# Halved first-layer weights, earlier key additions, and gate work moved across a phase border, in attention followed by a gated mixture of experts

## The chip, the cores and the metric

The kernel runs on one core of one Trainium2 chip. The metric is the device time of one execution in microseconds, given as the median of several runs. The core has five engines that run their own instruction streams: TensorE (PE, matmuls; PEld are its weight loads), VectorE (DVE), ScalarE (ACT), GpSimd (POOL) and SyncE (SP). In this kernel SyncE issues the plain transfers, and GpSimd issues those that change the type (the expert weights).

## The reference

Multi-query attention is computed first: 8 batches, 16 query heads over one key and value head, 384 tokens, head size 64. Its output is 3072 tokens of 1024 features. Each token then picks the best of 4 groups and the best of 4 experts in it, and passes one expert of two layers (1024 to 1024 to 1024); the result is scaled by the product of two softmax weights.

```python
scores = scale * np.matmul(q, k.transpose(0, 1, 3, 2))
scores = scores - np.max(scores, axis=-1, keepdims=True)
attn = np.exp(scores)
attn = attn / (np.sum(attn, axis=-1, keepdims=True) + 1e-09)
out = np.matmul(attn, v)
...
g_logits = x @ w_group                      # 4 groups
g_idx = np.argmax(g_logits, axis=1)
...
e_logits = xg @ w_expert[g]                 # 4 experts in the group
...
h = np.maximum(xg[mask_e] @ w1[g, e], 0.0)
ye = h @ w2[g, e]
out[tok_idx] = combined[:, None] * ye       # combined = g_w * e_w
```

## The kernel before

The kernel goes through 24 **phases**, `p = 3*b + st`: batch `b` (8 of them), tile `st` of 128 tokens (3 per batch). One phase computes the scores and exponentials of its own tile (six key blocks `j`), and the products with the values of the phase before, in turn. In the data most tokens of a batch go to one expert. So the kernel picks one expert per batch by the counts of the batch's first tile, loads its weights, and runs the whole batch through it, in 14 **units** per batch: 8 of the first layer (`h_unit`, 8 matmuls each) and 6 of the second (`y_unit`, 8 matmuls each). From phase 3 on, 4 or 5 such units follow the attention part of each phase (`fill`), as filling work for TensorE. What the chosen experts leave over is put right at the end with the "extra" pair of batch and expert.

Nearly all matmul results stand in one pool of three PSUM buffers, taken by `side`. A matmul that wants a buffer waits until its former content has been read. The instructions of each engine stand in the order in which the code emits them.

```python
ps_s = fast.enter_context(tc.psum_pool(name="ps_s", bufs=3))
ps_m = fast.enter_context(tc.psum_pool(name="ps_m", bufs=1))
...
def side(shape, dtype, name):
    return ps_s.tile(shape, dtype, tag="s", name=name)

def load_w1(w1, e):                       # 4 MB in DRAM, turned to bf16 on the way
    for a in range(2):
        nc.gpsimd.dma_start(out=w1[a * D:(a + 1) * D], in_=w1f[bass.ds(e, 1), a].rearrange("e p k f -> (e p) k f"))

def scores(p, j):
    ps = side([P, 2, CW], FP32, "s")
    ...                                   # 4 matmuls: s <- qT, kT
    nc.scalar.activation(out=t[:], in_=ps[:], func=ACTF.Exp, scale=scale)   # pt

def pre_add(p, j):                        # sum over the key blocks
    if j == 1:
        nc.vector.tensor_add(out=presum[p][:], in0=pt[p, 0][:], in1=pt[p, 1][:])
    else:
        nc.vector.tensor_add(out=presum[p][:], in0=presum[p][:], in1=pt[p, j][:])

# fold_keys(p): VectorE sums presum to 128 x 32 (fold)
# join(p):      4 small matmuls, sm <- fold
# invert(p):    VectorE reciprocal of sm, then spread over the tile by a transpose (rinv)
# values(p, j): 4 matmuls into o
# prep_q(p), prep_k(b): turn queries and keys by a VectorE transpose; turn_q does it on TensorE

def weigh(p):
    nc.vector.tensor_mul(out=xT[b][:, :, ts], in0=o_ps[p]..., in1=rinv[p]...)
    nc.gpsimd.tensor_copy(out=xbf[b][:, :, ts], in_=xT[b][:, :, ts])   # bf16 for the experts
    ...

def gate_a(b, lo, hi):                    # gate products: gps, copied by ScalarE to part
def gate_b(b, lo=0, hi=ST):               # lps <- part, sel
def choose_a(b, ps):                      # VectorE: best group and expert of the first tile
def choose_b(b):
    ps = side([P, GE], FP32, "c1ps")      # expert counts
    nc.tensor.matmul(out=ps[:], lhsT=ones_bf[:], rhs=first[b]..., start=True, stop=True)
    nc.vector.tensor_copy(out=cnt[:], in_=ps[:])
    nc.vector.max_with_indices(out_max=top[:], out_indices=idx[:], in_=cnt[:])
    reg = nc.values_load(idx[0:1, 0:1], engines=(ET.Pool,), ...)
    load_w1(w1, reg)
    nc.gpsimd.dma_start(out=w2[:], in_=w2f[bass.ds(reg, 1)]...)
    ...
def gate_c(b):                            # counts of all three tiles (cps), then gsel

def h_unit(fc):
    ps = side([P, CW], FP32, "hps")
    ...                                   # 8 matmuls: hps <- xbf, w1
    nc.scalar.activation(out=state["h"][:, fc, :], in_=ps[:, 0:S], func=ACTF.Relu)   # hT
def y_unit(st, nh):
    ps = side([P, CW], FP32, "yps")
    ...                                   # 8 matmuls: yps <- w2, hT
    nc.scalar.activation(out=y, in_=ps[:], func=ACTF.Copy, scale=gs_of()[:, st:st + 1])

# ---- the loop ----
for p in range(NP):
    b, st = divmod(p, ST)
    jobs = jobs_gates(0) if p == 2 else []
    ...
    for j in range(3):
        scores(p, j)
    ...                                   # prep_k, turn_q or prep_q
    for j in range(KB):
        if jobs: jobs.pop(0)()
        if p > 0: values(p - 1, j)
        if j == 2 and p > 0: join(p - 1)
        if j + 3 < KB: scores(p, j + 3)
        if j > 0: pre_add(p, j)
        if j == 2 and p > 0: invert(p - 1)
        if j == 3: stats_q(p)
        ...
    if p > 0: weigh(p - 1)
    fold_keys(p)
    ...                                   # st == 2: prep_k(b + 1), stats_k(b + 1)
    if p >= ST:
        jobs = []
        if st == 1: jobs = jobs_gates(b)  # gate_a; gate_b and the choice; the counts
        if p == NP - 1: jobs = [bound_a, bound_b]
        phase(5 if p in FIVES else 4, jobs)   # a unit, then from the second on also a job

join(NP - 1); ...                         # the tail: last values, last gates, 24 units left,
                                          # the extra pair: load_pair, ph <- w1c, py <- w2c
```

Of the kernel before, what the change touches and what calls it, by code (L numbers as in the profile page):

```python
# [21 lines left out]
def kernel(  # L22
# [11 lines left out]
    nc = tc.nc  # L34
    B, H, S, D = q.shape
# [3 lines left out]
    F = moe_w1.shape[3]  # L39
    assert S == 384 and D == 64 and Dm == 1024 and F == 1024 and N == B * S  # L40
    assert H == 16 and G == 4 and Eg == 4
    ST = S // P
# [10 lines left out]
    w1f = moe_w1.rearrange("g e (a ko d) f -> (g e) a d ko f", a=2, d=D)  # L53
# [3 lines left out]
    HC = CW // P  # L57
# [15 lines left out]
    def side(shape, dtype, name):  # L73
        return ps_s.tile(shape, dtype, tag="s", name=name)

    q_raw, k_raw, v_sb, kT, qT, pt, xT, xbf, gsel, wts = {}, {}, {}, {}, {}, {}, {}, {}, {}, {}

    q_todo = []
    q_nat = []
# [15 lines left out]
    def some_q(n=1):  # L95
        for _ in range(n):
            if q_todo:
                q_todo.pop(0)()
# [38 lines left out]
            q_nat.append(qe)  # L137

    def load_w1(w1, e):
        for a in range(2):  # L140
            nc.gpsimd.dma_start(out=w1[a * D:(a + 1) * D], in_=w1f[bass.ds(e, 1), a].rearrange("e p k f -> (e p) k f"))  # L141

    ones_bf = singles.tile([P, P], BF16, name="ones_bf")
    nc.vector.memset(ones_bf[:], 1.0)
# [45 lines left out]
    def load_gw():  # L190
        for a in range(2):
            rows = slice(a * D, (a + 1) * D)
            nc.sync.dma_start(out=gw[rows, :, 0:G], in_=moe_w_group.rearrange("(a ko d) g -> a d ko g", a=2, d=D)[a])
            for g in range(G):
                nc.sync.dma_start(out=gw[rows, :, G + g * Eg:G + (g + 1) * Eg], in_=moe_w_expert[g].rearrange("(a ko d) e -> a d ko e", a=2, d=D)[a])
# [6 lines left out]
    def stats_q(p):  # L202
        junk = pool.tile([P, 2 * CW], BF16, tag="junk", bufs=1, name="junk")
        nc.scalar.activation(out=junk[:].rearrange("p (h n) -> p h n", h=HP), in_=q_of(p), func=ACTF.Square, accum_out=stat_q[:, p:p + 1])  # L204
# [12 lines left out]
    def turn_q(p, nat, copies):  # L217
        qT[p] = pool.tile([P, 2 * CW], FP32, tag="qT", bufs=2, name="qT")
        n = HP // len(copies)
        for i, copy in enumerate(copies):  # L220
            ps = side([P, 2 * CW], FP32, "qps")
            for h in range(n):
                nc.tensor.transpose(out=ps[:, h * P:(h + 1) * P], in_=nat(i * n + h).rearrange("p a d -> p (a d)"), identity=ident[:])
            copy(out=qT[p][:, i * n * P:(i + 1) * n * P], in_=ps[:, 0:n * P])

    def prep_k(b):
        kT[b] = pool.tile([P, S], FP32, tag="kT", name="kT")
        nc.vector.transpose(out=kT[b][:], in_=k_raw[b][:].rearrange("p k d -> p (k d)"))

    def q_of(p):  # L230
        b, st = divmod(p, ST)
        if b == 0:
            return q_raw[0][:, st].rearrange("p h a d -> p h (a d)")
        return q_raw[b][:, :, st * (P // 32):(st + 1) * (P // 32)].rearrange("p h k d -> p h (k d)")

    def prep_q(p):
        qT[p] = pool.tile([P, 2 * CW], FP32, tag="qT", bufs=2, name="qT")
        nc.vector.transpose(out=qT[p][:].rearrange("p (h n) -> p h n", h=HP), in_=q_of(p))  # L238

    def scores(p, j):  # L240
        b = p // ST
        ps = side([P, 2, CW], FP32, "s")
        for c in range(2):
            for a in range(2):
                r = slice(64 * a, 64 * a + 64)
                nc.tensor.matmul(out=ps[64 * c:64 * c + 64, a, :], lhsT=kT[b][r, j * D:(j + 1) * D], rhs=qT[p][r, c * CW:(c + 1) * CW], start=True, stop=True)  # L246
        t = pool.tile([P, 2, CW], FP32, tag="pt", bufs=9, name="pt")
        nc.scalar.activation(out=t[:], in_=ps[:], func=ACTF.Exp, scale=scale)  # L248
        pt[p, j] = t

    def pre_add(p, j):
        if j == 1:
            presum[p] = pool.tile([P, 2, CW], FP32, tag="presum", bufs=1, name="presum")
# [3 lines that stand above are left out]
# [46 lines left out]
    def gate_a(b, lo, hi):  # L303
        n = (hi - lo) * P
        ps = side([P, CW], FP32, "gps")
        for r in range(2):
            for j in range(4):
                ko = 4 * r + j
                nc.tensor.matmul(out=ps[32 * j:32 * j + 32, 0:n], lhsT=gw[:, ko, :], rhs=xT[b][:, ko, lo * P:hi * P], start=(r == 0), stop=(r == 1), tile_position=(0, 32 * j))
        part[b] = part_all  # L310
        nc.scalar.copy(out=part[b][:, lo * P:hi * P], in_=ps[:, 0:n])

    def gate_b(b, lo=0, hi=ST):
        ps = side([P, ST, 32], FP32, "lps")
        for st in range(lo, hi):
            nc.tensor.matmul(out=ps[:, st, :], lhsT=part[b][:, st * P:(st + 1) * P], rhs=sel[:], start=True, stop=True)  # L316
        return ps
# [104 lines left out]
    def first_units(b):  # L422
        def place(st, cs):
            if done[0]:
                y = pool.tile([P, 2 * CW], FP32, tag="pt", bufs=9, name="yt")
            else:
                y = pool.tile([P, CW], FP32, tag="y", bufs=4, name="y")
            return y[:, 0:CW]

        def store(st, cs, y):  # L430
            nc.sync.dma_start(out=outv[b, :, st, cs], in_=y)
        return moe_units(wts[b][0], wts[b][1], xbf[b], lambda: gsel[b], place, store)

    NP = B * ST
# [3 lines left out]
    stats_k(0)  # L438
    turn_k_first()
    turn_q(0, lambda h: q_raw[0][:, 0, h], [nc.scalar.copy, nc.vector.tensor_copy])  # L440
    turn_q(1, lambda h: q_raw[0][:, 1, h], [nc.vector.tensor_copy])
    load_gw()

    units = []
# [2 lines left out]
    def fill(n):  # L447
        while n > 0:
            if not units:
                if begun[0] >= B or begun[0] not in wts:  # L450
                    return
                units.extend(first_units(begun[0]))
                begun[0] += 1
            units.pop(0)()
            n -= 1

    def phase(n, jobs):
        for i in range(n):
            fill(1)
            some_q()  # L460
            if i > 0 and jobs:
                jobs.pop(0)()
        while jobs:
            jobs.pop(0)()

    def gate_both(b):
        ps = gate_b(b)
        choose_a(b, ps)
        gate_logits(b - 1, ps, 1, ST)
        gate_math(b - 1)  # L470

    def count_both(b):
        choose_b(b)
        gate_c(b - 1)

    def jobs_gates(b):
        if b == 0:
            return [lambda: gate_a(0, 0, 1), lambda: choose_a(0, gate_b(0, 0, 1)), lambda: choose_b(0)]
        return [lambda: gate_a(b, 0, ST), lambda: gate_both(b), lambda: count_both(b)]

    bound = {}
    oki = singles.tile([1, 1], I32, name="oki")
# [20 lines left out]
    FIVES = (9, 13, 17, 20)  # L503
# [3 lines that stand above are left out]
        if st == 0 and b + 1 < B:  # L507
            load_q(b + 1)
        for j in range(3):
            scores(p, j)  # L510
        if p == 0:
            prep_k(1)
        elif p == 1:
            turn_q(2, lambda h: q_raw[0][:, 2, h], [nc.scalar.copy])
        elif p == 2:
            turn_q(3, lambda h: q_nat[h // HC][:, h % HC], [nc.scalar.copy])
        elif p < NP - 1:
            prep_q(p + 1)
        for j in range(KB):
            if jobs:  # L520
                jobs.pop(0)()
            if p > 0:
                values(p - 1, j)
            if j == 2 and p > 0:
                join(p - 1)
            if j + 3 < KB:
                scores(p, j + 3)
            if j > 0:
                pre_add(p, j)
            if j == 2 and p > 0:  # L530
                invert(p - 1)
            if j == 3:
                stats_q(p)
            if p < 4 and 0 < j < 5:
                some_q()
        assert not jobs
        if p > 0:
            weigh(p - 1)
        fold_keys(p)
        if st == 1 and b + 1 < B:  # L540
            if b > 0:
                load_k(b + 1)
            load_v(b + 1)
        if st == 2 and b + 1 < B:
            if b > 0:
                prep_k(b + 1)
            stats_k(b + 1)
        if p >= ST:
            jobs = []
            if st == 1:  # L550
                jobs = jobs_gates(b)
            if p == NP - 1:
                jobs = [bound_a, bound_b]
            phase(5 if p in FIVES else 4, jobs)

    done[0] = True
    join(NP - 1)
# [253 lines left out]
```

## Time and profile before

The median of 3 runs is 494.3 us (493.04 to 494.57). One profiled execution spans 491.4 us.

| part of the profile | before |
|---|---|
| TensorE clock granted, mean | 0.993 |
| scores, TensorE (L246), 1152 matmuls | 141.9 us busy |
| values, TensorE (L285), 1152 matmuls | 140.6 us busy |
| first expert layer (L401), 512 matmuls | 90.9 us busy |
| second expert layer (L409), 384 matmuls | 86.7 us busy |
| exponentials, ScalarE (L248), 144 | 142.1 us busy, 1026 ns each |
| key additions, VectorE (L254, L256), 120 | 145.7 us busy, 1215 ns each |
| weight transfers by GpSimd | 27, 37.84 MB written |

A line of the profile's time order reads: start in us, duration in us, engine, line of the kernel, operation, output and inputs by the names in the code, shapes, and the number of instructions merged; in square brackets stands the idle time of the engine before it and what ended it. A line of waits reads: engine, what waited, for whom, then the total in us, how often, and the longest. TensorE instructions are pipelined, so a merged group can seem longer than the distance to the next one; distances between starts are safer.

### The profile page before, as it was taken

The numbers are of one execution on the slowest core, as the hardware profiler recorded it, in microseconds if no ns is written. First come the engines' busy times: TensorE is split into PE (matmuls) and PEld (weight loads), VectorE is DVE, ScalarE is ACT, GpSimd is POOL, SyncE is SP. The second block draws the span as 40 slices with busy tenths as digits, with TensorE's granted clock in tenths as the row PEclk, the third lists the DMA queues.
The fourth block names the chain that finished last, engine by engine and source line by source line (L and its number), as shares of the span: only waits on it lengthen the run. The fifth ranks groups of instructions, "written<-read, shape, count | busy, mean of one in ns | idle before, by whom it ended". The sixth has DMA issues, their size and how long they took to land. (4 is left out here: it accounts for less than half of the span.)

```text
span 491.4 us, 9357 instructions
## 1 busy us (share of the span) xinstructions
PE 466.2 (95%) x3828; PEld 202.7 (41%) x3828; DVE 307.9 (63%) x487; ACT 247.8 (50%) x346; POOL 48.0 (10%) x64
## 2 busy tenths in 40 slices
PE   7999698999999998999999999999999999999993
PEld 6333244333344334434434334433434434445651
DVE  4779737856777847866677756855686675734200
ACT  2966263664456463565456464565465455423231
POOL 1002000200010000200010002000010002001000
PEclk9999899999999999999999999999999999999998
DMA  8797992996949595996789386977599303985990
GB/s 161 93 118 130 218 187 36 158 245 169 126 66 213 135 222 65 154 211 175 129 119 208 106 187 114 192 146 187 120 155 209 119 21 102 200 190 150 238 261 29
DMA packets 146242, 74.52 MB, mean 152 GB/s; under 512 B 120443, under 2 KB 120443, under 8 KB 146192
## 3 DMA queue, kind: packets, MB, share of 16 engines
q0 software_dynamic: 19008, 37.84, 42.6%
q1 hardware_dynamic: 126384, 35.81, 36.0%
q8 instruction: 32, 0.52, 0.4%
q10 hardware_dynamic: 800, 0.20, 0.2%
q14 instruction: 18, 0.15, 0.1%
HBM read 92.62 MB, written 19.40 MB: 228 GB/s over the span
## 5 line engine op out<-in xcount | busy, mean ns | idle before, releaser
L248 ACT ACTIVATE pt<-s 128x1024 f32<-128x1024 f32 x144 | 142.1, 1026 | 69.7 <-PE s L246 68.5
L246 PE MATMUL s<-qT,kT 64*64 64x512 f32 x1152 | 141.9, 595 | 2.3 <-ACT hT L402 1.7
L285 PE MATMUL o<-pt,v 64*64 64x512 f32 x1152 | 140.6, 590 | 1.2 <-DVE xT L296 1.2
L256 DVE TENSOR_TENSOR presum<-presum,pt 128x1024 f32<-128x1024 f32 x96 | 116.6, 1215 | 7.9 <-DVE presum L254 0.5
L401 PE MATMUL hps<-xbf,w 128*128 128x384 bf16 x512 | 90.9, 330 | 5.4 <-POOL xbf L297 5.0
L409 PE MATMUL yps<-w,hT 128*128 128x512 bf16 x384 | 86.7, 379 | 0.0
L285 PEld LDWEIGHTS o<-pt,v 64*64 64x64 f32 x1152 | 43.4, 133 | 78.7 <-issue 74.9
L401 PEld LDWEIGHTS <-w 128*128 128x128 bf16 x512 | 49.1, 100 | 50.3 <-issue 21.5
L254 DVE TENSOR_TENSOR presum<-pt 128x1024 f32<-128x1024 f32 x24 | 29.1, 1214 | 61.2 <-ACT pt L248 61.1
L402 ACT ACTIVATE hT<-hps 128x384 bf16<-128x384 f32 x64 | 31.3, 489 | 71.2 <-PE hps L401 71.1
L246 PEld LDWEIGHTS s<-qT,kT 64*64 64x64 f32 x1152 | 39.8, 133 | 63.6 <-issue 51.4
L297 POOL CAST xbf<-xT 128x1024 bf16<-128x1024 f32 x24 | 25.0, 1042 | 332.9 <-DVE xT L296 332.9
L409 PEld LDWEIGHTS <-hT 128*128 128x128 bf16 x384 | 36.3, 98 | 49.3 <-issue 8.9
L410 ACT ACTIVATE y<-yps,gsel 128x512 f32<-128x512 f32 x36 | 24.8, 688 | 48.9 <-PE yps L409 41.8
L296 DVE TENSOR_TENSOR xT<-o,rinv 128x1024 f32<-128x1024 f32 x24 | 29.2, 1218 | 3.6 <-PE o L285 3.6
L275 DVE STREAM_TRANSPOSE rinv<-rc 128x1024 f32<-128x1024 f32 x24 | 29.9, 1246 | 0.8
L260 DVE TRANSPOSE_TENSOR_REDUCE fold<-presum 128x32 f32<-128x1024 f32 x24 | 29.6, 1235 | 0.0
L273 DVE RECIPROCAL rc<-sm 128x32 f32<-128x32 f32 x24 | 8.6, 358 | 29.6 <-PE sm L268 29.5
L238 DVE STREAM_TRANSPOSE qT<-qraw 128x1024 f32<-128x1024 f32 x20 | 24.3, 1215 | 2.0 <-DMA qraw<-in_q_dram 1.7
L204 ACT ACTIVATE junk<-qraw 128x1024 bf16<-128x1024 f32 x21 | 22.0, 1049 | 0.0
L141 POOL DMA_DIRECT2D w<-in_moe_w_dram x18 | 12.6, 706 | 69.8 <-DVE gsel L389 43.5
L351 DVE COPY L<-lps 128x20 f32<-128x20 f32 (+1 forms) x16 | 3.0, 186 | 25.5 <-PE lps L316 25.5
(147 smaller groups left out, 187.9 us busy)
## 6 DMA issues: line engine op xcount, KB each, us to landing
w<-in_moe_w_dram POOLq DMA_DIRECT2D x18, 1024.0 KB, 12.9
w<-in_moe_w_dram POOLq DMA_DIRECT2D x9, 2048.0 KB, 23.9
qraw<-in_q_dram SPq DMA_DIRECT2D x56, 192.0 KB, 5.0
out_dram<-y SPq DMA_DIRECT2D x36, 256.0 KB, 4.4
x_bf<-xbf SPq DMA_DIRECT2D x8, 768.0 KB, 3.7
out_dram<-yt SPq DMA_DIRECT2D x12, 256.0 KB, 6.1
v<-in_v_dram SPq DMA_DIRECT2D x16, 96.0 KB, 2.6
k<-in_k_dram SPq DMA_DIRECT2D x28, 48.0 KB, 3.3
```

The source lines that it names most:

```text
L246: nc.tensor.matmul(out=ps[64 * c:64 * c + 64, a, :], lhsT=kT[b][r, j * D:(j + 1) * D], rhs=qT[p][r, c * CW:(c + 1) * CW], start=True, stop ...
L248: nc.scalar.activation(out=t[:], in_=ps[:], func=ACTF.Exp, scale=scale)
L254: nc.vector.tensor_add(out=presum[p][:], in0=pt[p, 0][:], in1=pt[p, 1][:])
L256: nc.vector.tensor_add(out=presum[p][:], in0=presum[p][:], in1=pt[p, j][:])
L260: nc.vector.tensor_reduce(out=fold[p][:], in_=presum[p][:].rearrange("p a (n i) -> p (a n) i", i=32), axis=AX, op=OP.add, apply_transpose= ...
L275: nc.vector.transpose(out=t[:].rearrange("p (b i) -> p b i", i=32), in_=rc[:].rearrange("p c b -> p (c b)").unsqueeze(2).to_broadcast([P, ...
L285: nc.tensor.matmul(out=o_ps[p][64 * a:64 * a + 64, c, :], lhsT=v_sb[b][r, j, :], rhs=pt[p, j][r, a, :], start=(j == 0), stop=(j == KB - 1))
L296: nc.vector.tensor_mul(out=xT[b][:, :, ts], in0=o_ps[p][:].rearrange("p c (h n) -> p (c h) n", n=P), in1=rinv[p][:].rearrange("p (h n) -> ...
L297: nc.gpsimd.tensor_copy(out=xbf[b][:, :, ts], in_=xT[b][:, :, ts])
L401: nc.tensor.matmul(out=ps[:, 0:S], lhsT=w1[:, ko, fc * P:(fc + 1) * P], rhs=xb[:, ko, :], start=(ko == 0), stop=(ko == KO - 1))
L402: nc.scalar.activation(out=state["h"][:, fc, :], in_=ps[:, 0:S], func=ACTF.Relu)
L409: nc.tensor.matmul(out=ps[:], lhsT=state["h"][:, fo, st * P:(st + 1) * P], rhs=w2[:, fo, nh * CW:(nh + 1) * CW], start=(fo == 0), stop=(fo ...
```

## The change

Four things are moved. Nothing is added or taken away in what is computed.

1. The first-layer weights `w1` are loaded in four transfers (two halves of F, each in two partition halves) in place of two, so that the first four units of a batch need the first half alone.
2. The key additions are emitted as their tiles appear: two ahead of the loop over `j`, three in it, two steps earlier than before. VectorE can then add while it would have waited for the join. At the start, the TensorE turns of the first queries are moved too: the second behind the first scores, the third and fourth from the head of their phases to the fourth step of the loop.
3. The gate products and the choice (`gate_a`, then `gate_b` with `choose_a`) come after the last two units of the phase with `st == 1`, in place of after the second and third.
4. The expert counts (`count_both`: `c1ps`, the index, the load of the weights, `cps`, `gsel`) leave that phase, and come first in the filling part of the next one (`st == 2`), ahead of its units.

```diff
     def load_w1(w1, e):
-        for a in range(2):
-            nc.gpsimd.dma_start(out=w1[a * D:(a + 1) * D], in_=w1f[bass.ds(e, 1), a].rearrange("e p k f -> (e p) k f"))
+        for c in range(2):
+            fs = slice(c * F // 2, (c + 1) * F // 2)
+            for a in range(2):
+                nc.gpsimd.dma_start(out=w1[a * D:(a + 1) * D, :, fs], in_=w1f[bass.ds(e, 1), a, :, :, fs].rearrange("e p k f -> (e p) k f"))
...
     turn_q(0, lambda h: q_raw[0][:, 0, h], [nc.scalar.copy, nc.vector.tensor_copy])
-    turn_q(1, lambda h: q_raw[0][:, 1, h], [nc.vector.tensor_copy])
...                        # phase() is taken out; its loop stands below
-        return [lambda: gate_a(b, 0, ST), lambda: gate_both(b), lambda: count_both(b)]
+        return [lambda: gate_a(b, 0, ST), lambda: gate_both(b)]
...
         for j in range(3):
             scores(p, j)
+            if p == 0 and j == 0:
+                turn_q(1, lambda h: q_raw[0][:, 1, h], [nc.vector.tensor_copy])
         if p == 0:
             prep_k(1)
-        elif p == 1:
-            turn_q(2, lambda h: q_raw[0][:, 2, h], [nc.scalar.copy])
-        elif p == 2:
-            turn_q(3, lambda h: q_nat[h // HC][:, h % HC], [nc.scalar.copy])
-        elif p < NP - 1:
+        elif 2 < p < NP - 1:
             prep_q(p + 1)
+        if jobs:
+            jobs.pop(0)()
+        for j in (1, 2):
+            pre_add(p, j)
         for j in range(KB):
-            if jobs:
-                jobs.pop(0)()
             if p > 0:
                 values(p - 1, j)
             if j == 2 and p > 0:
                 join(p - 1)
             if j + 3 < KB:
                 scores(p, j + 3)
-            if j > 0:
-                pre_add(p, j)
+            if 0 < j < 4:
+                pre_add(p, j + 2)
             if j == 2 and p > 0:
                 invert(p - 1)
             if j == 3:
                 stats_q(p)
+                if p == 1:
+                    turn_q(2, lambda h: q_raw[0][:, 2, h], [nc.scalar.copy])
+                elif p == 2:
+                    turn_q(3, lambda h: q_nat[h // HC][:, h % HC], [nc.scalar.copy])
+            if jobs:
+                jobs.pop(0)()
...
         if p >= ST:
-            jobs = []
+            n = 5 if p in FIVES else 4
+            if st == 2 and b > 0:
+                count_both(b)
+            steps = {}
             if st == 1:
-                jobs = jobs_gates(b)
+                gate_a_, gate_b_ = jobs_gates(b)
+                steps = {n - 2: gate_a_, n - 1: gate_b_}
             if p == NP - 1:
-                jobs = [bound_a, bound_b]
-            phase(5 if p in FIVES else 4, jobs)
+                steps = {1: bound_a, 2: bound_b}
+            for i in range(n):
+                fill(1)
+                some_q()
+                if i in steps:
+                    steps[i]()
```

More of the change, by code (lines that the diff above doesn't have):

```diff
@@ L455, in fill @@
             n -= 1
[L457 to L461, printed above, removed]
-                jobs.pop(0)()
-        while jobs:
-            jobs.pop(0)()
     def gate_both(b):
@@ L510 @@
             scores(p, j)
+            if p == 0 and j == 0:
+                turn_q(1, lambda h: q_raw[0][:, 1, h], [nc.vector.tensor_copy])
         if p == 0:
             prep_k(1)
-        elif p == 1:
-            turn_q(2, lambda h: q_raw[0][:, 2, h], [nc.scalar.copy])
-        elif p == 2:
-            turn_q(3, lambda h: q_nat[h // HC][:, h % HC], [nc.scalar.copy])
-        elif p < NP - 1:
+        elif 2 < p < NP - 1:
             prep_q(p + 1)
+        if jobs:
+            jobs.pop(0)()
+        for j in (1, 2):
+            pre_add(p, j)
         for j in range(KB):
-            if jobs:
-                jobs.pop(0)()
             if p > 0:
```

## The prediction

> **What bounds the kernel now.** I read the busy shares first, then TensorE's own waits, then TensorE in order of time, then VectorE in two stretches, and last the DMA in windows of 3 us near the end.
>
> ```profile
> PE 466.2 (95%) x3828; PEld 202.7 (41%) x3828; DVE 307.9 (63%) x487; ACT 247.8 (50%) x346; POOL 48.0 (10%) x64
> ```
>
> TensorE works 466.2 of 491.4 us, so a change that adds no matmuls can win or lose only in TensorE's gaps, 25 us, and in cold clock. Some 7.8 us of them lie behind the last matmul (483.6). The waits (total, times, longest) name most of the others:
>
> ```profile
> PE hps L401 <- POOL xbf L297: 5.0, 2, 4.3
> PE cps L378 <- DVE ohe L365: 2.8, 6, 0.5
> PE s L246 <- ACT hT L402: 1.7, 5, 0.3
> PE gps L309 <- ACT hT L402: 1.7, 3, 0.6
> PE o L285 <- DVE xT L296: 1.2, 1, 1.2
> ```
>
> The 4.3 us is the first expert matmul, at 57.12. Its weights are not late: the weight load in front of it ran at 53.25. It waits for GpSimd's cast (56.02, 1.04 us), and that for VectorE, which from 37 us on has no gap:
>
> ```profile
> 49.81 1.25 DVE L275 STREAM_TRANSPOSE rinv<-rc 128x1024 f32<-128x1024 f32 x1
> 50.98 3.84 DVE L256 TENSOR_TENSOR presum<-presum,pt 128x1024 f32<-128x1024 f32 x3
> 54.74 1.22 DVE L296 TENSOR_TENSOR xT<-o,rinv 128x1024 f32<-128x1024 f32 x1
> 55.88 1.24 DVE L260 TRANSPOSE_TENSOR_REDUCE fold<-presum 128x32 f32<-128x1024 f32 x1
> ```
>
> So phases 1 to 3, which have no expert units, are bound by VectorE. From phase 4 on TensorE is the bound, and VectorE finishes some 2 us behind it in each phase. The phase with st = 2 of batch 1, whose values end on TensorE at 94.40, shows that:
>
> ```profile
> 86.06 1.25 DVE L238 STREAM_TRANSPOSE qT<-qraw 128x1024 f32<-128x1024 f32 x1
> 91.06 0.36 DVE L273 RECIPROCAL rc<-sm 128x32 f32<-128x32 f32 x1 [1.31 <-PE sm L268]
> 92.62 3.84 DVE L256 TENSOR_TENSOR presum<-presum,pt 128x1024 f32<-128x1024 f32 x3
> 96.39 1.22 DVE L296 TENSOR_TENSOR xT<-o,rinv 128x1024 f32<-128x1024 f32 x1
> 98.68 0.53 DVE L228 STREAM_TRANSPOSE kT<-k 128x384 f32<-128x384 f32 x1
> ```
>
> At the end the DMA matters (window: us, busy of each engine, clock, DMA share, GB/s):
>
> ```profile
> 432.00:435.00 3.00, 3.00 (x27) 1.08 (x20) 0.81 (x1) 0.00 (x0) 0.00 (x0) 1.00 1.13 214
> 441.00:444.00 3.00, 3.00 (x16) 1.38 (x15) 1.78 (x12) 1.05 (x2) 0.00 (x0) 1.00 0.00 0
> 477.00:480.00 3.00, 3.00 (x58) 3.00 (x56) 0.00 (x0) 0.94 (x2) 0.00 (x0) 1.00 0.89 313
> 480.00:483.00 3.00, 3.00 (x17) 1.27 (x15) 0.00 (x0) 1.29 (x2) 0.00 (x0) 1.00 0.04 16
> ```
>
> The last batch's weights (issued at 414.05) keep the queues full till about 439; then comes a lull; then the extra pair's weights, issued from 448.61 and 452.7 and landing up to 26.6 us later (tile view), so at about 479.3. The last matmuls `py`, which need them, begin at 479.98: 0.7 us to spare.
>
> [...]after the gap of 4.3 us the windows 58 to 62 show clock 0.52 and 0.63, and the first 32 expert matmuls took 6.97 us (57.12 to 64.09), where 40 later ones take 6.61 (at 313), so 32 take 5.3; after the gap of 1.2 us at 43.6 nothing of the kind. [...]weights alone fill the share to 1.1 at 200 to 214 GB/s. So splitting by F gives order, not speed.
>
> **The change part by part.**
> *Halves of F.* 36 issues of 0.7 us on GpSimd for 18; GpSimd is 10% busy. No expert matmul of before waited for weights: 0.
>
> *Start.* The second query turn moves behind the first scores, so TensorE no longer stands 1.2 us for that query (9.20), but ScalarE's exponentials follow at 0.92 us each, and I get only about 0.8 us on VectorE's first sum.
>
> *Key additions.* In phase 1 VectorE stood 0.83 us for `sm`, in phase 2 2.14 us for `lps`, with additions it could have done. From the first sum of phase 1 (21.25 before, 20.2 now) I walk the new order with the trace's pitches: addition 1.25, reciprocal 0.39, spread 1.17, weighing 1.14, fold 1.16, first choice 1.3, turn 1.15. A phase is 10.15. Phase 2 starts at 30.3 and ends at 41.8 (before 45.78); phase 3 needs 1.15 + 4x1.25 + 1.56 + 1.25 + 1.14 = 10.1, so the weighing ends at 52.0 and the cast at 53.15. The first expert matmul moves from 57.12 to 53.2: **-3.9**. TensorE stands about 3.1 us instead of 4.3[...]: of the 1.7 us of cold clock I count 1.0 as won, **-1.0**. In phase 6 the wait of 0.7 for the cast goes, **-0.7**.
>
> *Gate products last.* gps 1.7, cps 2.8, and scores or hps behind them 1.7 + 0.6 go: **-6.8**, because VectorE's choice now runs under three scores (2.6 us), and the cast is done before the products.
>
> *Counts first.* This puts something new on the path. In the next phase `c1ps` and `cps` take two of the three `side` buffers at T0, when the values end, and give them back only when VectorE has copied the counts. VectorE's order there is: rest of the gate chain (2.85 after `lps`; the next time is counted from the first score), query turn, four additions, reciprocal and spread, one addition, weighing, fold, key turn, then the copies. That is 3.05 + 1.17 + 5.03 + 1.56 + 1.26 + 1.13 + 1.16 + 0.54 = 14.9, while T0 is 94.40 - 83.82 = 10.6 after the first score. So the first buffer comes back at T0 + 4.5, the second at T0 + 5.1. Between them the expert units have one buffer. In the program as built the unit after the first waits either for the evacuation of the unit before (0.2 to start, 0.49 to run, 0.07 to be seen: 0.76 us) or for the copy. Counted over batches 1 to 7: nine waits of the first kind, 6.8; of the second, batch 1 2.6 (its second unit), batches 5 and 6 1.0 each, batch 7 0.5 (no key turn). Sum **+11.9**.
>
> *Later weights.* The loads of each batch are issued behind the counts, so about 14 us later. Batches 1 to 6 still have over 20 us to their first unit against some 13 for the first matrix: 0. For batch 7 the issue moves from 414 to about T0 + 6 = 428 (T0 = 422.4), its transfer ends near 454, not 439, and the lull is used up. The pair's weights queue behind it: by the work left in the windows (14.3 later, less 7.5 us of lull share) up to 6.8 us later, of which TensorE is itself 1.4 later and had 0.7 to spare; a count by transfer gives 2. I take **+4** with some cold clock.
>
> Sum: 494.3 - 3.9 - 1.0 - 0.7 - 6.8 + 11.9 + 4 = 497.8. I take 497, since the positive terms rest on more links than the negative ones.
>
> **The rivals.**
> 1. The counts' buffers cost nothing (VectorE is ahead of where I put it, as the additions now come earlier). For: the additions do fill VectorE's 1.31 us wait for `sm`. Against: that 1.31 is smaller than the 2.85 of gate chain that now lies in the same phase. If so, 494.3 - 12.4 + 4 = 486, or 482 without the tail.
> 2. The tail is hidden: the pair's transfer keeps its place, or its last part isn't what `py` waits for. For: the DMA rates in the windows go from 167 to 313 GB/s, so the queue may catch up. Against: 0.7 us of slack. Then 494.
> 3. The tail is worse: 1 KB pieces slow the queue, [...]`py` runs at half clock. Against: nothing in the profile of before measures smaller pieces. Then 501 to 503.
> 4. VectorE gains nothing in phases 1 to 3, as additions wait for exponentials there. Against: two tiles of phase 2 stand ready at 30.8, while VectorE adds them only from 35.20. Then 501.
>
> **Range and chances.** One standard error of the counts' term is about 3 us, of the tail 2.5, of the start 1.5, so 4.2 together; 8 times in 10 that is 491 to 502.5. Faster by over 2% needs less than 484.4, which asks for rival 1 and rival 2 together: 0.06. Slower by over 2% needs 504.2: 0.06. Within 2%: 0.88.
>
> **What would show it.** In the changed trace: first expert matmul at 52 to 54 with a TensorE wait of 2.5 to 3.5 us for the cast; no wait for `ohe`, hardly any for `gps`; in each phase with st = 2 a new wait of `hps` or `yps` for `hT` (about 0.76 each) or for `cnt` (2.6 in batch 1), some 12 us in all; VectorE's `cnt` copies 4 us behind the values' end; the last batch's weights issued 6 us behind the values of phase 23, and a wait of `py` of 2 to 5 us for `w` near the end. I am wrong if the waits for `cnt` and `hT` in these phases stay below 6 us, if `py` doesn't wait, or if the first expert matmul stays at 56 or later.

## The result, and the profile after

The changed kernel takes **513.3 us** (512.2 to 514.8), against 494.0 for the kernel before on the same chip: a ratio of 1.040, interval 1.036 to 1.043. It is slower by 4%, and the prediction's range ended at 502.5. The profiled executions span 511.9 and 491.4 us, TensorE's mean clock is 0.973 and was 0.993.

From the page of the changed kernel, the busy shares; then TensorE's waits and one of VectorE's (total, times, longest):

```profile
PE 475.5 (93%) x3828; PEld 204.8 (40%) x3828; DVE 305.8 (60%) x487; ACT 247.2 (48%) x346; POOL 60.2 (12%) x82
```

```profile
PE hps L403 <- DVE rc L275: 9.6, 5, 3.6
PE py L710 <- DMA w<-in_moe_w_dram: 5.2, 1, 5.2
PE hps L403 <- ACT hT L404: 4.6, 8, 0.6
PE hps L403 <- POOL xbf L299: 3.2, 1, 3.2
PE yps L411 <- DVE cnt L338: 2.4, 1, 2.4
PE hps L403 <- DVE cnt L338: 1.7, 1, 1.7
...
PE yps L411 <- ACT hT L404: 0.6, 1, 0.6
```

```profile
DVE qT L240 <- DMA qraw<-in_q_dram: 15.2, 5, 4.8
```

The matmuls are the same 3828, yet TensorE is busy 9.3 us longer. Most of that is cold clock: in the traces' clock records TensorE worked 20.5 us at half clock, and 3.4 before, which makes 8.5 us (an estimate: half of the difference). The wait for `ohe` is gone, those of `gps` are down to 0.4 us, and waits for `cnt` and `hT`, and of `py`, have come, all foreseen in kind. The largest is one that the prediction did not name: five times `hps` waits for the reciprocal `rc`, 9.6 us. And VectorE waits 15.2 us for queries, where before it waited 1.7.

Where the 20.5 us of span come from, by phase (distance between the first scores of one phase and the next, after less before):

| part of the span | after less before, us |
|---|---|
| start to the end of phase 3 | -3.3 |
| seven phases with st = 1 (gate products last) | -9.6 |
| phases 6, 9, ... 21 | -0.9 |
| six phases with st = 2, batches 1 to 6 | **+26.4** |
| phase 23 and the tail | +7.9 |

Phase 14 shows what goes wrong. TensorE there, in order of time:

```profile
257.42 2.32 PE L287 MATMUL o<-pt,v 64*64 64x512 f32 x19
259.67 0.18 PE L336 MATMUL c1ps<-ohe,ones_bf 128*128 128x16 bf16 x1
259.71 0.18 PE L380 MATMUL cps<-ohe,ones_bf 128*128 128x48 bf16 x1
262.21 2.72 PE L403 MATMUL hps<-xbf,w 128*128 128x384 bf16 x8 [2.32 <-DVE rc L275]
265.51 1.46 PE L403 MATMUL hps<-xbf,w 128*128 128x384 bf16 x8 [0.58 <-ACT hT L404]
```

The two count products take two of the three buffers. The third still holds `sm`, the softmax sums, until VectorE has inverted them. So the first unit stands 2.32 us, and then its 8 matmuls take 2.72 us where the next 8 take 1.46: the clock has fallen to half and come back (window: us, busy, clock, DMA share, GB/s):

```profile
260.00:262.00 2.00, 0.00 (x0) 0.00 (x0) 1.90 (x3) 0.00 (x0) 0.00 (x0) 1.00 0.00 0
262.00:264.00 2.00, 1.79 (x6) 0.86 (x6) 1.97 (x3) 0.00 (x0) 0.00 (x0) 0.51 0.00 0
```

Why is the inversion late? VectorE in the same phase:

```profile
255.54 1.25 DVE L240 STREAM_TRANSPOSE qT<-qraw 128x1024 f32<-128x1024 f32 x1 [3.50 <-DMA qraw<-in_q_dram]
256.71 1.18 DVE L256 TENSOR_TENSOR presum<-pt 128x1024 f32<-128x1024 f32 x1
258.00 3.89 DVE L258 TENSOR_TENSOR presum<-presum,pt 128x1024 f32<-128x1024 f32 x3
261.80 0.35 DVE L275 RECIPROCAL rc<-sm 128x32 f32<-128x32 f32 x1
...
267.21 0.14 DVE L338 COPY cnt<-c1ps 128x16 f32<-128x16 f32 x1
```

It stands 3.50 us for the next phase's queries, and the additions and the reciprocal stand behind that turn. Without those 3.5 us the reciprocal would, by these lines, have started at 258.3, ahead of the values' end (an estimate). And why are the queries late? SyncE's issues of the changed kernel (start, time that the issue took, what), and below them those of the kernel before at the same place:

```profile
226.20 0.44 SPq L89 DMA_DIRECT2D qraw<-in_q_dram  x1
226.73 9.48 SPq L433 DMA_DIRECT2D out_dram<-y  x1
236.26 0.42 SPq L89 DMA_DIRECT2D qraw<-in_q_dram  x1
236.78 3.17 SPq L433 DMA_DIRECT2D out_dram<-y  x1
...
247.20 4.05 SPq L89 DMA_DIRECT2D qraw<-in_q_dram  x4
```

```profile
226.28 0.86 SPq L89 DMA_DIRECT2D qraw<-in_q_dram  x1
227.23 1.45 SPq L431 DMA_DIRECT2D out_dram<-y  x1
...
241.72 3.93 SPq L89 DMA_DIRECT2D qraw<-in_q_dram  x4
```

The first query piece is issued at the same time, but its landing comes at 240.5 instead of 231.1, and the store of `y` behind it takes 9.48 us to issue instead of 1.45, though ScalarE had finished its `y` at 226.70. All later pieces wait in SyncE's order behind that store. VectorE's turn starts when the last piece has landed, at 255.3. This piece took 5.2 us to land, as before (5.1), but the last four were issued from 247.20 on instead of 241.72. So here it is the held issues, not the slower transfers, that make the queries late; in the other four waits of VectorE the last piece also took 4.9 to 5.4 us. The difference is what else flows: the last weights of batch 3 were issued at 198.1 before and had landed at 221.9; now they are issued at 214.0 and land at 239.7. Between 226 and 240 the DMA share is 1.10 to 1.23, where before it was 0.43 from 236 on, and the first query piece takes 14.2 us to land instead of 4.8. Why the issue itself stands, no run shows, and no run takes the stores out of SyncE's order.

My theory at this point: each half of the +26.4 is one cause. The held buffers cost about what was predicted. The later weights run while the next batch's queries go out, VectorE waits for those, and with all three buffers held TensorE waits for VectorE. The rivals: the half loads, the new order of additions, or the tail's own load.

### The profile page after: what moved, and what is told of

The parts are those of the page before. It is cut to its first block, busy times and chain, and to the rows that moved or that the text cites. A ratio compares the mean times of both kernels' runs of the same rounds, so it can differ in the third digit from the quotient of the medians.

```text
span 511.9 us, 9399 instructions
## 1 busy us (share of the span) xinstructions
PE 475.5 (93%) x3828; PEld 204.8 (40%) x3828; DVE 305.8 (60%) x487; ACT 247.2 (48%) x346; POOL 60.2 (12%) x82
## 5 line engine op out<-in xcount | busy, mean ns | idle before, releaser
L403 PE MATMUL hps<-xbf,w 128*128 128x384 bf16 x512 | 95.3, 339 | 19.1 <-DVE rc L275 9.6
L411 PE MATMUL yps<-w,hT 128*128 128x512 bf16 x384 | 88.2, 384 | 3.0 <-DVE cnt L338 2.4
L403 PEld LDWEIGHTS <-w 128*128 128x128 bf16 x512 | 50.4, 101 | 65.0 <-issue 37.3
L240 DVE STREAM_TRANSPOSE qT<-qraw 128x1024 f32<-128x1024 f32 x20 | 24.5, 1225 | 15.2 <-DMA qraw<-in_q_dram 15.2
L143 POOL DMA_DIRECT2D w<-in_moe_w_dram x36 | 24.8, 707 | 34.1 <-PE yps L411 12.4
L412 ACT ACTIVATE yt<-yps,gsel 128x512 f32<-128x512 f32 x12 | 8.2, 687 | 15.7 <-PE yps L411 13.2
```

The costliest lines, as they stand in the source:

```text
L403: nc.tensor.matmul(out=ps[:, 0:S], lhsT=w1[:, ko, fc * P:(fc + 1) * P], rhs=xb[:, ko, :], start=(ko == 0), stop=(ko == KO - 1))
L411: nc.tensor.matmul(out=ps[:], lhsT=state["h"][:, fo, st * P:(st + 1) * P], rhs=w2[:, fo, nh * CW:(nh + 1) * CW], start=(fo == 0), stop=(fo ...
```

## The experiments

Eleven kernels ran, each against the kernel before on the same chip. By the same parts of the span, less before. These parts are those of one profiled execution of each kernel; the phases 6, 9, ... 21 are left out (-0.9, but -0.3 in e4 and +0.5 in e6). The profiled execution can lie off the median: that of e8 took 497.3 us, 3.2 above it, and that of e2 483.3, about 2 below. The start also varies with the clock in phase 3, by up to 2.9 us (the first 32 expert matmuls took 5.36 us in e2 and 8.28 in e9; last section):

| run | time, us | ratio (interval) | start | st = 1 | st = 2 | tail |
|---|---|---|---|---|---|---|
| after | 513.3 | 1.040 (1.036 to 1.043) | -3.3 | -9.6 | +26.4 | +7.9 |
| e1, whole `w1` loads | 513.5 | 1.043 (1.040 to 1.046) | -3.8 | -9.6 | +26.6 | +8.3 |
| e2, gates and counts back | 485.2 | 0.985 (0.983 to 0.987) | -5.3 | -2.1 | 0.0 | -1.4 |
| e3, one load of weights | 492.6 | 0.999 (0.998 to 1.000) | -3.9 | -9.6 | +13.7 | +0.6 |
| e4, query turn late | 504.2 | 1.022 (1.020 to 1.024) | -1.9 | -9.6 | +17.7 | +6.5 |
| e5, counts behind tile 1 | 489.0 | 0.990 (0.989 to 0.992) | -2.8 | -9.6 | +8.8 | +0.8 |
| e6, gates and counts alone | 515.8 | 1.045 (1.044 to 1.047) | -0.1 | -9.6 | +23.3 | +9.1 |
| e7, last counts early | 507.7 | 1.031 (1.028 to 1.034) | -3.4 | -9.6 | +26.6 | +0.9 |
| e8, late loads alone | 494.1 | 1.002 (1.001 to 1.004) | -2.7 | -2.1 | +5.7 | +4.4 |
| e9, counts behind tile 2 | 483.6 | 0.979 (0.976 to 0.981) | -2.3 | -9.6 | +3.8 | -0.1 |
| e10, counts behind tile 3 | 487.9 | 0.990 (0.988 to 0.991) | -5.1 | -9.6 | +8.5 | +0.5 |
| e11, e9 with fillers | **480.6** | 0.975 (0.974 to 0.976) | -5.2 | -9.6 | +3.4 | -0.2 |

**e1: the halves of F undone.**

```diff
-        for c in range(2):          # two halves of F, each in two partition halves
...
+        for a in range(2):          # as before: two transfers
...
```

> The changed kernel, but each first-layer matrix loaded in two transfers as before. Theory (the loss comes from the moved counts and the later loads that collide with the queries; the halves of F do nothing): 513 us, within 1.5 of the changed kernel, the same waits for rc, cnt, hT. Rival (the 1 KB pieces slow the queue, so that queries and the pair's weights come late): 505 to 509, wait of py for w under 3 us in place of 5.2.

513.5 us, with nearly the same waits (`rc` 11.3, `py` 4.9). The halves do nothing that shows; the tail's loss is not from smaller pieces.

**e2: gates and counts at their old places**, so that only the halves, the additions and the query turns stay changed.

```diff
-        return [lambda: gate_a(b, 0, ST), lambda: gate_both(b)]
+        return [lambda: gate_a(b, 0, ST), lambda: gate_both(b), lambda: count_both(b)]
...
-            if st == 2 and b > 0:
-                count_both(b)
...
-                steps = {n - 2: gate_a_, n - 1: gate_b_}
+                steps = {1: gate_a_, 2: gate_b_, 3: count_}
```

> The changed kernel with the gate products and the counts back at their old places; the additions, the turns and the halves of F stay. Theory: the start keeps its 3.3 us, gps and the cast give 2 to 3 more, all waits for rc, cnt and hT in the phases with st = 2 go, py doesn't wait: 487 to 490. Rival (the additions ahead of the reciprocal hold the join's buffer too long and are to blame): over 500, with waits for rc left.

485.2 us, 1.8 under the expected range, and 1.5% faster than before. The phases with st = 2 are those of before to 0.01 us. Its TensorE waits keep the old ones for the gates:

```profile
PE cps L380 <- DVE ohe L367: 2.8, 6, 0.5
PE s L248 <- ACT hT L404: 1.7, 5, 0.3
```

So the new order of the additions, together with the query turns at the start, is a gain by itself (no run parts the two), and the whole loss lies in the moved gates and counts. That it is the counts, and not the gates, e9 shows below: there the gates stay moved.

**e3: the changed kernel with the first batch's weights used for all batches**; the loads of batches 1 to 7 are left out, so the output is another one.

```diff
+        if b == 0:
             w1 = wpool.tile(...); load_w1(w1, reg); w2 = ...; wts[b] = (w1, w2)
+        else:
+            wts[b] = wts[0]
```

> The changed kernel with the weight loads of batches 1 to 7 left out (all run on the matrices of batch 0; the counts, the index and the extra pair's load stay). It separates the two halves of the loss. Theory (the waits for rc come from queries that arrive late behind the weights; the buffers held by the counts cost about what was predicted): waits for rc under 1.5 us in all in place of 9.6, no idle of VectorE for the queries in place of 15.2, py doesn't wait, but nine waits of 0.6 to 0.8 for hT and about 4 us for cnt stay: 494 to 498. Rival (buffers alone make the loss, whatever the transfers do): 506 or more with the waits for rc left. Second rival (all the loss is transfers): 488 or less.

```profile
PE hps L406 <- ACT hT L407: 4.6, 8, 0.6
...
PE hps L406 <- DVE cnt L338: 2.9, 2, 1.7
PE yps L414 <- DVE cnt L338: 2.3, 1, 2.3
...
PE yps L414 <- ACT hT L407: 0.6, 1, 0.6
```

492.6 us, 1.4 under the expected range. No wait for `rc` is left, and the waits for buffers, 10.4 us, are nearly as they were (9.3). The phases with st = 2 lose 13.7 us and the tail 0.6. The store behind the first query piece issues in 1.43 us again:

```profile
222.18 0.85 SPq L89 DMA_DIRECT2D qraw<-in_q_dram  x1
223.13 1.43 SPq L436 DMA_DIRECT2D out_dram<-y  x1
```

So 12.7 us of st = 2 and 7.3 of the tail come with the weights' transfers, and 14 without them.

**e4: the query turn behind the last addition**, so that late queries hold up neither additions nor reciprocal.

```diff
-        elif 2 < p < NP - 1:
-            prep_q(p + 1)
...
+                elif 2 < p < NP - 1:      # in the loop, at j == 3
+                    prep_q(p + 1)
```

> The changed kernel with VectorE's turn of the next queries moved from the head of a phase to behind the last addition, so that VectorE no longer stands for queries that are on their way. Theory (late queries hold up VectorE, VectorE holds up the reciprocal, the reciprocal a buffer): waits for rc under 2 us in place of 9.6 and some 4 us of cold clock less, tail as in the changed kernel: 498 to 503. Rival (it is the order of reciprocal and additions): waits for rc stay above 6 us, 509 or more.

504.2 us, just above the expected range. The wait for `rc` is gone, but the late queries now hold up the weighing and the copies behind it, and the waits for `cnt` grow from 4.1 to 11.1:

```profile
PE hps L403 <- DVE cnt L338: 6.1, 4, 1.5
PE yps L411 <- DVE cnt L338: 5.0, 2, 3.1
PE py L710 <- DMA w<-in_moe_w_dram: 4.9, 1, 4.9
```

It moves the wait from one buffer to the two others; the cause is ahead of both.

**e6: gates and counts alone.** The kernel before with parts 3 and 4 of the change; loads, query turns and additions as before (the diff is that of parts 3 and 4).

> The kernel before with only the move of the gate products and of the counts; first-layer weights in two transfers, query turns and key additions as before. Theory: the move of the counts alone makes the loss. No gain at the start (first expert matmul at 57), so the sum is 494 - 10 (gates) + 18 to 26 (phases with st = 2) + 8 (tail) = 508 to 518 us; VectorE's wait for queries is 10 us or more, py waits about 5 us. Since here only one addition stands ahead of the reciprocal, the wait of hps for the reciprocal may be smaller than the 9.6 us of the changed kernel; the wait for cnt should then be larger than 4.1. Rival (the new order of the additions is what makes the counts costly): 494 or less, no reciprocal wait, cnt and hT below 6 us together.

515.8 us, within the expected range, and slower than the changed kernel, since the gain at the start is missing. The new order of the additions is cleared. With two additions ahead of the reciprocal instead of four (the expectation says one; in the trace there are two), the wait for `rc` is 4.9 us instead of 9.6 although VectorE waits 22.2 us for queries; the waits for `cnt` and `hT` are larger instead, 5.6 and 8.7 us in all:

```profile
PE hps L401 <- ACT hT L402: 7.5, 13, 0.6
...
PE hps L401 <- DVE rc L273: 4.9, 3, 3.8
PE yps L409 <- DVE cnt L336: 4.4, 2, 3.0
```

**e8: late loads without held buffers.** The kernel e2, with only the loads of batches 1 to 7 issued one phase later, behind GpSimd's cast.

```diff
     def choose_b(b):
         ...                                # counts and index, where they were
-        reg = nc.values_load(idx...); load_w1(w1, reg); ...
+    def choose_c(b):                       # register and loads
+        reg = nc.values_load(idx...); load_w1(w1, reg); ...
...
+            if st == 2 and b > 0:
+                choose_c(b)
```

> The kernel with gates and counts at their old places (485.2 us), but with the weights' transfers of batches 1 to 7 issued one phase later, behind GpSimd's cast in the phase with st = 2, so at about the place where the changed kernel issues them; no buffer is held there. It shows the transfers' lateness alone. Theory: the queries of the next batch land 8 to 14 us later, VectorE stands for them 8 to 15 us in all, hps waits for the reciprocal at least 5 us in all, py waits for weights 3 us or more: 496 to 506 us. Rival (late transfers alone are harmless, only together with held buffers do they cost): 485 to 488 us, or 489 to 492 with the tail, and no reciprocal wait.

494.1 us, 8.9 more than e2: between the theory's 496 to 506 and the rival's 485 to 492. The first half of the theory stands: VectorE waits even longer for queries (first line, its waits), and `py` waits. The second half does not, as it was put: no `hps` waits for `rc`. What waits is the next phase's first scores, for the key turn at the end of VectorE's list (TensorE's waits):

```profile
DVE qT L240 <- DMA qraw<-in_q_dram: 20.3, 5, 4.9
```

```profile
PE s L248 <- DVE kT L230: 5.3, 5, 1.6
...
PE py L715 <- DMA w<-in_moe_w_dram: 3.1, 1, 3.1
```

With free buffers TensorE works on through its units while VectorE catches up: 20.3 us of VectorE's wait cost the phases with st = 2 only 5.7. The two causes are not additive. Alone they cost these phases 13.7 (e3) and 5.7 (e8), together 26.4; the 7 us in between need both. Some 4 of them are cold clock (an estimate): in the changed kernel TensorE worked 7.9 us at half clock in phases 14 and 17, in e3 and e8 not at all there.

**e7: the counts early in the last batch alone** (the edit is that of e5, for b = 7 only).

> The changed kernel, but with the counts early (behind the first values of the phase) for the last batch alone; batches 1 to 6 are as in the changed kernel. Theory: the last phase and the tail, which lost 7.9 us, lose at most 1 us: the last weights are issued some 8 us earlier, and py waits for weights less than 0.7 us; the other phases stay as they were. Time 505 to 507.5 us. Rival (the tail's loss is not from the last load's place but from the pair's own load): py still waits 4 us or more, 510 us or more.

507.7 us, 0.2 above the expected range. Phase 23 and the tail lose 0.9 us instead of 7.9, and `py` no longer waits; its 16 matmuls take 3.61 us, where in the changed kernel they took 6.45 after their gap of 5.25. The tail's loss is the place of the last load.

**e5, e9, e10: the counts early in the phase, at three places.** The gate products stay last in the phase before.

```diff
             if j + 3 < KB:
                 scores(p, j + 3)
+            if j == 1 and st == 2 and b > 0:       # e9; e10: j == 2
+                count_both(b)                      # e5: j == 0, and the query turn and two additions behind it
...
-            if st == 2 and b > 0:
-                count_both(b)
```

> The changed kernel, but in the phases with st = 2 the two count products are issued right behind the first values of the phase, ahead of the query turn and of the additions, instead of behind the values' end. Theory (counts at the phase's end hold two of three buffers and send the weights 14 us later into the query loads): VectorE copies the counts some 5 us into the phase, before any expert unit asks for a buffer, and the weights are issued 8 to 9 us earlier than in the changed kernel. Then no wait of hps or yps for cnt or hT in these phases, at most 1 us in all of the reciprocal, VectorE's wait for queries below 4 us in all instead of 15, no wait of py for weights; the phases with st = 2 are as long as before to 0.5 us each, while the gates keep their gain of 1.1 to 1.7 us in each phase with st = 1. Time 478 to 484 us. Rival 1 (the order of additions and reciprocal makes the loss, wherever the counts stand): 500 or more, with the reciprocal's wait still there. Rival 2 (the gate products last in a phase cost as much as they win): about 485, the time of the kernel with gates and counts at their old places.

> The changed kernel, but in the phases with st = 2 the two count products stand behind the values of the second key tile, and VectorE's copies of them behind the query turn and two additions. Theory: VectorE gets there 6.7 us into the phase and TensorE at about 6.4, so neither waits for the other (with the counts behind the first tile VectorE stood 12.0 us for them and the scores stood 4.9 us for the key turn); the buffers are back before the values' end, the weights are issued 5 to 7 us earlier than in the changed kernel. No wait of hps or yps for cnt or rc, s for kT at most 1.5 us, py none; phases with st = 1 keep their gain, phases with st = 2 at most 0.6 us over before: 478 to 483 us. Rival (the gates' rest on VectorE makes every phase with st = 2 too long wherever the counts stand): kT wait stays at 4 us or more, 486 to 490.

> As the run with the counts behind the second key tile, but behind the third. Theory: still before the values' end, so no wait for cnt; VectorE copies 8 to 8.5 us into the phase; the weights are issued 1.2 us later than there, which costs nothing or, through the queries and the tail's py, up to 3 us: 478 to 486 us. Rival as there: kT wait 4 us or more, 486 to 490.

e5 takes 489.0 us, 5 above the expected range: the buffers and the weights are cured, but VectorE reaches the counts before TensorE has made them, stands for them (first line), and pays it back at the key turn:

```profile
DVE cnt L338 <- PE c1ps L336: 12.0, 7, 1.7
```

```profile
PE s L248 <- DVE kT L230: 4.9, 5, 1.8
```

e9 moves them behind the second tile, where both engines arrive together (VectorE of phase 11, with no bracket on its lines: no idle time):

```profile
189.70 1.25 DVE L240 STREAM_TRANSPOSE qT<-qraw 128x1024 f32<-128x1024 f32 x1
...
192.15 1.23 DVE L258 TENSOR_TENSOR presum<-presum,pt 128x1024 f32<-128x1024 f32 x1
193.30 0.17 DVE L338 COPY cnt<-c1ps 128x16 f32<-128x16 f32 x1
```

The product `c1ps` ran at 192.94 there. No `hps`, `yps` or `py` waits for counts, inversions or weights any more, and the time is 483.6 us, 0.6 above the expected range. The 3.8 us that its phases with st = 2 still lose are mostly the count products themselves, about 0.6 us a phase, which have come from the phases before. e10, one tile later, takes 487.9. That is above the expected range and inside the rival's, but the rival's sign, a wait for `kT`, is missing: `cps` then wants a buffer that still holds scores, and stands for their exponential:

```profile
PE cps L380 <- ACT pt L250: 5.4, 5, 1.1
```

**e11: e9 with 24 idle matmuls in the gap of phase 3**, which nothing reads. The same gap had cost e2 nothing and e9 up to 2.9 us.

```diff
+            if p == ST:
+                keep = side([P, CW], FP32, "keep")
+                for _ in range(24):
+                    nc.tensor.matmul(out=keep[:, 0:P], lhsT=ones_bf[:], rhs=ones_bf[:], start=True, stop=True)
```

> The kernel with the counts behind the second key tile, with 24 idle matmuls (ones by ones, 128 columns, nothing reads them) behind the values of phase 3, so that TensorE's gap of 3.2 us before the first expert unit is cut to about 1.4. Theory (the gap of 3.2 us sometimes costs nothing and sometimes up to 2.9 us of cold clock, since the first 32 expert matmuls took 5.36 us in one profile and 8.28 in another after the same gap): these 32 take 5.3 to 5.5 us at clock 1.00, phase 3 loses nothing to the fillers, and the time is 479.5 to 482.5 us, with less spread than the 480.5 to 484.1 of the kernel without fillers. Rival (the long first unit is from weights that land late, not from the clock): they still take over 7 us and the time stays at 483 to 484.

The first expert matmuls in three kernels: after, e2, e11.

```profile
53.89 6.98 PE L403 MATMUL hps<-xbf,w 128*128 128x384 bf16 x32 [3.19 <-POOL xbf L299]
```

```profile
53.51 5.36 PE L403 MATMUL hps<-xbf,w 128*128 128x384 bf16 x32 [3.19 <-POOL xbf L299]
```

```profile
50.34 1.51 PE L553 MATMUL keep<-ones_bf 128*128 128x128 bf16 x24
53.60 5.36 PE L403 MATMUL hps<-xbf,w 128*128 128x384 bf16 x32 [1.75 <-POOL xbf L299]
```

480.6 us (480.3 to 481.6, where e9 ran from 480.5 to 484.1): the fastest of all by its median, 2.5% under the kernel before. The fillers lie in a gap, so they cost nothing, and behind them the first 32 expert matmuls take 5.36 us, as in e2. The mean clock of its five executions is 0.996 to 0.998, of e9's 0.989 to 0.996.

## Why the prediction was wrong

**The step that failed** is "Later weights": "Batches 1 to 6 still have over 20 us to their first unit against some 13 for the first matrix: 0." The loads are indeed in time for the units. But that asked only who waits for the weights, not whom they delay. In place of 0 the transfers cost the phases of batches 1 to 6 12.7 us (26.4 less the 13.7 of e3): queries late by SyncE's held issues, VectorE 15.2 us behind them, then the reciprocal, the third buffer, and TensorE's clock. None of my four rivals had it.

The other steps, by the runs:

- **Halves of F, 0**: right (e1).
- **Start, -3.9 and -1.0**: the first expert matmul moved from 57.12 to 53.89, so -3.2. The cold clock was not won in the changed kernel (6.98 us for the first 32, 6.97 before), but in e2 it was (5.36). The 1.0 was an estimate; the gap was 3.19 us in both (last section). Where the clock held, in e2, the start is -5.3, near the sum of the two terms, -4.9.
- **Cast in phase 6, -0.7**: -0.9.
- **Gate products last, -6.8**: right in kind. The seven phases are 9.6 us shorter, in e6 too, without the new additions. By e11's 0.6 us a phase, some 4 of these may be the count products, which left for the next phase (an estimate). The additions alone give 2.1 there (e2), but not on top of the 9.6.
- **Counts first, +11.9**: right in kind and nearly in size. The waits for `hT` and `cnt` are 5.2 and 4.1 us in the changed kernel, 10.4 together in e3, where the nine waits for `hT` are as counted, at 0.58 us instead of 0.76. There, without the transfers, the phases with st = 2 and the tail lose 14.3 in all. The term had left out the count products themselves, 3.4 us in six phases by e11, and cold clock in phase 5, where TensorE worked 3.4 us at half clock.
- **The tail, +4**: right in kind (e7), too small by about 3: `py` waited 5.25 us, just above the 2 to 5 named, but then ran cold, 6.45 us against 3.62 (clock 0.50 from 497.5 to 504.4). That half of rival 3 came true, without its 1 KB pieces (e1). With the 7.3 us that go with the transfers, the term should have been 7.

With 12.7 for the 0 and 7.3 for the 4, the prediction's sum of 497.8 becomes 513.8. That it comes so near to 513.3 is in part luck: the other errors (1.6 us less won at the start, 2.8 more by the gates, 2.4 more lost by the counts) nearly cancel.

Rival 1, buffers that cost nothing since VectorE is early, is refuted by e3: with no late queries, 10.4 us of waits for buffers stay. Rivals 2 and 4 fell too: `py` waited, and the additions, with the turns, did win at the start. The share of busy time did not warn: VectorE fell from 63% to 60% as it became the one that TensorE waits for.

## What to carry to other kernels

When a load moves in time, ask two questions: is it still there when it is needed, and what flows at its new place that had the queues for itself. A small product that takes a buffer should stand where its reader arrives at the same time: one tile too early the reader stands (e5), one too late the buffer is still held (e10), at the end of the list everyone stands (after). Two causes that each look cheap, a held buffer and a late engine, can cost more together than their sum, as here (13.7 and 5.7 us alone, 26.4 together), since each uses up slack that hid the other, and since TensorE's clock fell to half behind the longer gaps (2.32 and 3.59 us in phases 14 and 17 of the changed kernel).

## What the runs showed of the hardware

- A store of `y` took 9.48 us to issue on SyncE (9.14 in e8) while a batch's weights were flowing from GpSimd's queue, 1.43 with these loads left out (e3), and 1.45 where they had landed 5 us before (before). The query piece behind it in SyncE's order, itself 0.42 us, was issued at 236.26, right after the 9.48 us had passed.
- TensorE's clock fell to half behind some gaps and not behind others, even of the same length (next lines and table).

The same gap of 3.19 us before the first expert matmul left the clock at 1.00 in e2 and was followed by half clock in e9 and in the changed kernel. Five gaps, with the expert matmuls behind them:

| gap | first matmuls behind it | clock behind it (window, us) |
|---|---|---|
| e2, phase 3, 3.19 us | 32 in 5.36 us | 1.00 (54 to 56) |
| e9, phase 3, 3.19 us | 32 in 8.28 us | 0.50 (54 to 56) |
| after, phase 3, 3.19 us | 32 in 6.98 us | 0.50 (54 to 56) |
| after, phase 11, 2.06 us | 8 in 1.46 us | 1.00 (204 to 206) |
| after, phase 14, 2.32 us | 8 in 2.72 us | 0.51 (262 to 264) |

So in these traces the length of a gap does not tell by itself what the clock does: 3.19 us went both ways, and the shorter 2.32 us was followed by half clock. What else decides was not shown; no run was made for it. In e11 the fillers leave a gap of 1.75 us, and in its one trace the first 32 expert matmuls took 5.36 us. That the clock would hold there in every execution is not shown.
